# Sliding-window attention with global tokens, then a cosine MLP: the global score products of two pairs formed one slot earlier

## Chip, cores and metric

One of the cores of a Trainium2 chip runs the whole program. The metric is the device time of one execution in microseconds: 959.86 us, the median of three (959.55 to 961.06). The engines are named as the profile names them: PE (matmuls), PEld (PE's weight loads), DVE, ACT, POOL and SP, whose queue issues every DMA.

## What is computed

Eight batches, eight heads of 64, 512 local positions and 32 global ones. Global queries attend to everything; a local query sees the 32 global keys and the local keys within 32 positions. The attention output, 4352 rows of 512, goes through an MLP with the activation h·cos(h):

```python
s_g = scale * np.matmul(q_g, k_all.transpose(0, 1, 3, 2))
out_g = np.matmul(sm(s_g), v_all)
s_ll = np.where(np.abs(pos[:, None] - pos[None, :]) <= 32, s_ll, -1e9)
out_l = np.matmul(sm(np.concatenate([s_lg, s_ll], -1)), v_all)
h = x @ w_in
return (h * np.cos(h)) @ w_out
```

## The kernel before

Two heads make a *pair*, so a batch has four pairs. Two pairs, an even one and the odd one behind it, make a *group*, whose global queries are handled together.

The MLP is the backbone. Rows of x are taken in 17 chunks of 256; each chunk goes through eight *slots*, in each of which PE forms 256 columns of h (`m1_a`, L801, 24 matmuls into the PSUM tile `ph`) and multiplies the 256 columns of three slots earlier with w_out (`m2_a`, L860 to L862, 12 matmuls into `po`). Everything is held as the sum of two fp16 parts, hence three matmuls for each product. Between the two, ACT, DVE and POOL form the activation: `u` (L823 on ACT, L824 on DVE), its sine `w` (L425 on ACT), the square (L839 on POOL), `gf` (L841 on DVE), and its parts `gh` (L845 on ACT) and `gl` (L846 on POOL).

The attention of the batches is woven into these slots. A pair of batch 2 or later has a base slot t, 16 slots to a batch and four to a pair, and a table of offsets says what it does when:

- t-10: its queries and keys are loaded (`load_qk`, tile `qkr`, three buffers).
- t-7 and t-5: local scores (`sc_a`, L527). Each call makes two `ps` tiles, one for each head. DVE takes them out of PSUM, two instructions at L545 to a tile, with the row minimum `mn`.
- t-4: the exponentials on ACT (`sc_c`), and behind them those of the group's global scores `gt` if the pair is odd (`g_c`). Both go through L425, as the sine does, and each change between exponential and sine loads a table (ACT_TABLE_LOAD).
- t-3: the weights are scaled and split (L592 on ACT, L593 on DVE) into `planes`; of the global ones L709 to L721 make `planes_g`.
- t-1: SP transposes both by DMA (`pt` at L612, `ptg` at L725).
- t: the product with the values (`av_a`, 36 matmuls at L645 into `acc`), taken out by `xh` (L665, ACT) and `xl` (L666, DVE).
- t+2, odd pairs: the global product (`g_f`, L737, `gacc`), taken out at L750.
- The global scores of a group (`g_a`, L682, tile `gps`; taken out by DVE at L695) come in two calls, 288 and 256 keys wide, whose slots `s_gs0` and `s_gs1` set.

The tiles `ps`, `gps`, `acc`, `gacc` and a small one for the spread of a maximum (`pm`, L459) share one PSUM tag, `att`, with three buffers that are handed out in turn, in the order in which the program makes the tiles. So PE may write a tile only when the third tile before it has been taken out of PSUM.

The values of a whole batch come by one load (`load_v`, L446, tile `vr`, one buffer) at slot t-12 of its first pair, which is the slot in which L512 reads the last piece of the batch before. DVE then takes the maximum over them (`v_a`, L481, `vm`).

The calls of each slot are handed to a scheduler in the order of phases; it may move an instruction a little, so the order on each engine is read from the built program. Each engine executes its own list in that order.

Of the kernel before, what the change touches and what calls it, by code (L numbers as in the profile page):

```python
# [78 lines left out]
s_tr = -1  # L79
s_vd = -8  # L80
s_av = 0
s_gs0 = -6
s_gs1 = -4
s_gd = -3
s_ge = -1
s_gf = 2
# [998 lines left out]
```

## Time and profile before

| | before |
|---|---|
| median of 3 | 959.86 us |
| the profiled execution, and its span | 959.23 us, 957.5 us |
| PE busy | 909.4 us, 95% of the span |
| ACT busy | 668.4 us, 70% |
| DVE busy | 569.3 us, 59% |
| POOL busy | 399.7 us, 42% |
| DMA, the one queue of SP | 39.6% of 16 engines |

The profile is of one execution; its own time is 1.7 us over its span, and 0.6 us under the median. A page and several views of the trace are used: the timeline (start, duration, engine, line, operation, tiles, and in brackets idle time before it and what ended it), the waits (who waited for whom), the chain of work that ended last (start, duration, engine and line, with consecutive pieces merged), stretches of time with busy times by engine, and the DMAs. Busy times of PE are modelled ends of pipelined matmuls, so for PE the text uses the starts of matmuls.

### The profile page before, as it was taken

To read this page: it belongs to the slowest core of one execution; us is meant where nothing else is said; L and a number is where in the kernel's file an instruction comes from. 1 tells how busy PE (TensorE), PEld (TensorE's weight loads), DVE (VectorE), ACT (ScalarE), POOL (GpSimd) and SP (SyncE) were. 2 spreads that over 40 slices of the span, in tenths; PEclk is the share of its full clock that TensorE was granted. 3 is DMA by queue.
4 is the path that set the end of the run, shared out by engine and by line. 5 is a ranking of instruction groups with operands and counts; after the bars stand their busy time and mean duration, and the time that the engine had idled before them with its cause. 6 is when DMAs were issued, how large, how long until landed. Compare 5 with 4: busy or idle time off the path is not lost.

```text
span 957.5 us, 20487 instructions
## 1 busy us (share of the span) xinstructions
PE 909.4 (95%) x7963; PEld 604.0 (63%) x7963; DVE 569.3 (59%) x1544; ACT 668.4 (70%) x1435; POOL 399.7 (42%) x412
## 2 busy tenths in 40 slices
PE   6657989999999999999999999999999999999995
PEld 4446656656666666666666666666666666766663
DVE  5987978746565656566655656564746554423231
ACT  7886899957787677766777778777777775443341
POOL 5856654443334243434343333324343434444441
PEclk8667989999999999999999999999999999999998
DMA  9936167745232533545262725342443333000000
GB/s 371 386 121 198 34 163 162 152 111 125 49 108 43 157 63 71 108 122 111 56 122 50 183 46 129 46 146 46 119 61 71 81 68 58 23 1 23 1 24 22
DMA packets 155178, 96.44 MB, mean 101 GB/s; under 512 B 141000, under 2 KB 141128, under 8 KB 153288
## 3 DMA queue, kind: packets, MB, share of 16 engines
q1 hardware_dynamic: 155080, 95.13, 39.6%
q8 instruction: 62, 1.02, 0.4%
q14 instruction: 36, 0.29, 0.1%
HBM read 51.59 MB, written 8.91 MB: 63 GB/s over the span
## 4 chain that ended last, share of the span: by engine, by line
PE 51%; ACT 15%; DVE 11%; issue 9%; POOL 8%; DMA 5%; SPq 0%; ACTq 0%; POOLq 0%; DVEq 0%
PE ph L801 21%; PE po L861 8%; PE po L862 8%; PE po L860 8%; ACT t L425 4%; DMA vr<-v 3%; POOL w L839 3%; PE ps L527 3%; POOL gl L846 2%; ACT planes L592 2%; PE acc L645 2%; DVE gf L841 2%; ACT gh L845 2%; ACT L425 2%; POOL wi_l L213 2%
## 5 line engine op out<-in xcount | busy, mean ns | idle before, releaser
L801 PE MATMUL ph<-xh,wi_h 128*128 128x256 f16 x1024 | 280.7, 274 | 0.9 <-DVE gf L841 0.5
L801 PE MATMUL ph<-xl,wi_h 128*128 128x256 f16 x1024 | 279.8, 273 | 0.0
L801 PE MATMUL ph<-xh,wi_l 128*128 128x256 f16 x1024 | 279.8, 273 | 0.0
L846 POOL TENSOR_TENSOR gl<-gf,gh 128x512 f16<-128x512 f32 x136 | 163.4, 1202 | 237.1 <-ACT gh L845 237.0
L839 POOL TENSOR_TENSOR w<-w 128x512 f32<-128x512 f32 x136 | 143.6, 1056 | 259.1 <-ACT w L425 241.2
L801 PEld LDWEIGHTS <-wi_h 128*128 128x128 f16 x2176 | 205.9, 98 | 55.4 <-issue 18.8
L861 PE MATMUL po<-wo_hl,gh 128*128 128x512 f16 x544 | 206.7, 380 | 0.6 <-POOL wo_hl L213 0.6
L860 PE MATMUL po<-wo_hl,gh 128*128 128x512 f16 x544 | 204.7, 380 | 1.7 <-ACT wo_hl L239 1.7
L862 PE MATMUL po<-wo_hl,gl 128*128 128x512 f16 x544 | 206.3, 380 | 0.0
L845 ACT CAST gh<-gf 128x512 f16<-128x512 f32 x136 | 83.4, 615 | 112.8 <-DVE gf L841 112.7
L824 DVE SCALAR_TENSOR_TENSOR u<-u,cm,ph 128x512 f32<-128x512 f32 x136 | 101.1, 744 | 101.0 <-ACT u L823 101.0
L841 DVE SCALAR_TENSOR_TENSOR gf<-w,ph 128x512 f32<-128x512 f32 x136 | 93.1, 684 | 110.6 <-POOL w L839 110.1
L425 ACT ACTIVATE w<-u,ca 128x512 f32<-128x512 f32 x136 | 98.1, 722 | 84.4 <-DVE u L824 83.5
L425 ACT ACTIVATE t<-t,mn 128x192 f32<-128x192 f32 (+1 forms) x256 | 117.3, 463 | 18.5 <-DVE mn L545 18.1
L801 PEld LDWEIGHTS <-wi_l 128*128 128x128 f16 x1088 | 106.7, 98 | 13.4 <-issue 0.5
L823 ACT ACTIVATE u<-ph,cm 128x512 f32<-128x512 f32 x136 | 92.3, 679 | 25.2 <-PE ph L801 25.2
L593 DVE SCALAR_TENSOR_TENSOR planes<-t,sm,planes 128x192 f16<-128x192 f32 (+1 forms) x232 | 97.8, 481 | 12.0 <-ACT planes L592 11.2
L545 DVE CUSTOM_DVE_ANT_0 t<-ps,msk 128x192 f32<-128x192 f32 (+1 forms) x256 | 83.2, 367 | 18.0 <-PE ps L527 14.8
L862 PEld LDWEIGHTS <-gl 128*128 128x128 f16 x544 | 53.3, 98 | 63.1 <-issue 0.9
L592 ACT ACTIVATE planes<-t,sm 128x192 f16<-128x192 f32 (+1 forms) x232 | 86.3, 458 | 0.0
L861 PEld LDWEIGHTS <-gh 128*128 128x128 f16 x544 | 53.3, 98 | 51.5 <-issue 2.5
L860 PEld LDWEIGHTS <-gh 128*128 128x128 f16 x544 | 52.8, 98 | 51.4 <-issue 2.6
(149 smaller groups left out, 1098.5 us busy)
## 6 DMA issues: line engine op xcount, KB each, us to landing
qkr<-qf SPq DMA_DIRECT2D x31, 608.0 KB, 5.0
vr<-v SPq DMA_DIRECT2D x8, 1280.0 KB, 6.5
out<-o SPq DMA_DIRECT2D x34, 256.0 KB, 2.0
raw_wi<-wi SPq DMA_DIRECT2D x6, 1024.0 KB, 12.2
wo_hl<-wo SPq DMA_DIRECT2D x8, 512.0 KB, 12.7
raw_wm<-wo SPq DMA_DIRECT2D x8, 512.0 KB, 5.7
raw_wo<-wo SPq DMA_DIRECT2D x8, 512.0 KB, 4.4
raw_wi<-wi SPq DMA_DIRECT2D x4, 512.0 KB, 12.3
```

Source lines behind the costliest of these rows:

```text
L425: ins = nc.scalar.activation(*a, **k).ins
L592: a = nc.scalar.activation(hi, t[:, h], AF.Identity, scale=r)
L593: d = nc.vector.scalar_tensor_tensor(lo, t[:, h], r, hi, op0=ALU.mult, op1=ALU.subtract)
L801: nc.tensor.matmul(ph[:, a], w[:, kc, f], x[:, kc, q], start=first and ip == 0, stop=last and ip == 2, skip_group_check=True,)
L824: nc.vector.scalar_tensor_tensor(u, u, m, ph, op0=ALU.subtract, op1=ALU.subtract)
L839: nc.gpsimd.tensor_tensor(w, w, w, op=ALU.mult)
L841: nc.vector.scalar_tensor_tensor(gf, w, 0.5, st.pop(("ph", c, j)).rearrange("p a b -> p (a b)"), op0=ALU.subtract, op1=ALU.mult,)
L845: nc.scalar.copy(gh, gf)
L846: nc.gpsimd.tensor_tensor(gl, gf, gh, op=ALU.subtract)
L860: nc.tensor.matmul(po[k], gh[:, q], wo_h[:, f], start=(f == 0), stop=False)
L861: nc.tensor.matmul(po[k], gh[:, q], wo_l[:, f], start=False, stop=False)
L862: nc.tensor.matmul(po[k], gl[:, q], wo_h[:, f], start=False, stop=(f == NJ - 1))
```

## The change

```diff
 s_av = 0
-s_gs0 = -6
-s_gs1 = -4
+s_gs0 = -7
+s_gs1 = -5
 s_gd = -3
```

Both calls of `g_a` move one slot forward for batches 2 to 7, two groups each, twelve groups in all. At t-7 and t-5 they stand directly behind the odd pair's own local scores; until now the first stood alone in t-6, ahead of the global product of the group before, and the second stood in t-4 behind `av_a` of the even pair.

The tiles with the tag `att` are made in this order for an odd pair and the even one that follows (| between slots). Before: ps ps | gps0 gacc | ps ps | acc gps1, then ps ps | ps ps | acc. After: ps ps gps0 | gacc | ps ps gps1 | acc, then ps ps | ps ps | acc. Counted three back, the second global tile `gps1` took the buffer of the first `ps` of its t-5 pair before, and takes that of `gacc` now; `acc` took the buffer of `gacc` before, and takes that of that first `ps` now; `gps0` takes the buffer of the even pair's `acc` (slot t-8) in both.

On PE, in batch 3 at the first odd pair, this is the end of the t-4 slot before (`acc_3_0` is the even pair's product, `ps_3_1_2_0` in the next lists is the first of the two score tiles of t-5):

```order
L645 LDWEIGHTS vl_3_0_3757
L645 MATMUL acc_3_0_4412<-pt_3_0_4347,vl_3_0_3757 64x128
L682 MATMUL gps_3_0_1_4449<-qkr_3_0_3585 32x256 [waits DVE_49]
L682 MATMUL gps_3_0_1_4449<-qkr_3_0_3585 32x256
L682 MATMUL gps_3_0_1_4449<-qkr_3_1_3906 32x256 x2
L801 LDWEIGHTS wi_h_86
L801 MATMUL ph_4_4_4482<-xh_2_3046,wi_h_86 128x256
```

The product runs first, and the global scores behind it wait for DVE. After, in the t-5 slot of the same pair:

```order
L527 MATMUL ps_3_1_2_0_4341<-qkr_3_1_3906 128x224 [waits DVE_49]
L527 MATMUL ps_3_1_2_1_4342<-qkr_3_1_3906 128x224 [waits DVE_49]
L527 MATMUL ps_3_1_2_0_4341<-qkr_3_1_3906 128x192
L527 MATMUL ps_3_1_2_1_4342<-qkr_3_1_3906 128x192
L682 MATMUL gps_3_0_1_4347<-qkr_3_0_3585 32x256 [waits DVE_49]
L682 MATMUL gps_3_0_1_4347<-qkr_3_0_3585 32x256
L682 MATMUL gps_3_0_1_4347<-qkr_3_1_3906 32x256 x2
```

The same four matmuls now follow the local scores. One slot later PE begins the product after with this:

```order
L801 LDWEIGHTS wi_h_86
L801 MATMUL ph_4_4_4482<-xh_2_3046,wi_h_86 128x256
L645 LDWEIGHTS vh_3_0_3756 [waits DMAHW3_49]
L645 MATMUL acc_3_0_4418<-pt_3_0_4352,vh_3_0_3756 64x128 [waits DVE_49]
L645 LDWEIGHTS vh_3_0_3756
```

Its first matmul waits for DVE, where before it waited for an earlier matmul of PE.

On DVE, the list at that place before. `vm_4` is the maximum over the values of the next batch, and the two L545 instructions on `ps_3_1_2_0` are those that take the first score tile of t-5 out of PSUM:

```order
L786 TENSOR_SCALAR co_6_5489<-osc_96,pvs_98 128x1 [waits DVE_49,Activation_49]
L481 TENSOR_REDUCE vm_4_4864<-vr_4_4729 128x1 [waits DMAHW7_49]
L545 ISA t_3_1_2_4352,mn_3_1_2_4353<-ps_3_1_2_0_4341,msk_73 128x224 [waits PE_49]
L545 ISA mn_3_1_2_4353 128x1
L545 ISA t_3_1_2_4352,mn_3_1_3_4356<-ps_3_1_2_0_4341,msk_73 128x192
L545 ISA mn_3_1_3_4356 128x1
L841 SCALAR_TENSOR_TENSOR gf_4_2_4365<-w_4_2_4322,ph_4_2_4296 128x512 [waits Pool_49]
```

And after:

```order
L786 TENSOR_SCALAR co_6_5489<-osc_96,pvs_98 128x1 [waits DVE_49,Activation_49]
L481 TENSOR_REDUCE vm_4_4872<-vr_4_4729 128x1 [waits DMAHW7_49]
L545 ISA t_3_1_2_4357,mn_3_1_2_4358<-ps_3_1_2_0_4341,msk_73 128x224 [waits PE_49]
L545 ISA mn_3_1_2_4358 128x1
L545 ISA t_3_1_2_4357,mn_3_1_3_4361<-ps_3_1_2_0_4341,msk_73 128x192
L545 ISA mn_3_1_3_4361 128x1
L841 SCALAR_TENSOR_TENSOR gf_4_2_4371<-w_4_2_4322,ph_4_2_4296 128x512 [waits Pool_49]
```

These rows stand as they did: the maximum, which waits for a load, stays ahead of them. The instructions on `gps` (L695) move forward on DVE with their matmuls, each to a place behind the L545 instructions of its slot.

On ACT the exponential of the global scores moves ahead of the scaling. Before, in the same pair:

```order
L665 ACTIVATE xh_3_4455<-acc_3_0_4412,xs_90 128x512 [waits PE_49]
L592 ACTIVATE planes0_76<-t_3_1_0_4141,sm_3_1_4463 128x192 [waits DMAHW3_49,DVE_49,Activation_49]
...
L592 ACTIVATE planes3_82<-t_3_1_2_4352,sm_3_1_4463 128x192 [waits Activation_49]
L425 ACTIVATE gt_3_0_4221,gsm_3_0_4472<-gt_3_0_4221,gmn_3_0_4222 128x544 [waits DVE_49]
L425 ACT_TABLE_LOAD
L425 ACTIVATE w_4_3_4395<-u_4_3_4394,ca_4_4078 128x512 [waits Pool_49]
```

After:

```order
L425 ACTIVATE gt_3_0_4154,gsm_3_0_4472<-gt_3_0_4154,gmn_3_0_4155 128x544 [waits DVE_49]
L665 ACTIVATE xh_3_4455<-acc_3_0_4418,xs_90 128x512 [waits PE_49]
L425 ACT_TABLE_LOAD [waits DVE_49]
L425 ACTIVATE w_4_3_4401<-u_4_3_4400,ca_4_4078 128x512 [waits Pool_49]
L592 ACTIVATE planes0_76<-t_3_1_0_4146,sm_3_1_4463 128x192 [waits DMAHW3_49,DVE_49,Activation_49]
```

The exponential, the table load and the next sine now precede the eight scalings, so L593, L612 and the transposes of `planes` come later, and POOL's square of that sine earlier. On POOL the last step of `planes_g` (L721) moves ahead of that square, and on SP the transpose of `planes_g` moves ahead of the four of `planes`. The loads of queries and keys keep their place on SP; they wait for the last reader of their buffer, which is a call of `g_a`.

## The prediction

> **What bounds the kernel now.** The page comes first, for which engine has no idle time and where; then one stretch of time for the part that the change can reach.
>
> ```profile
> PE 909.4 (95%) x7963; PEld 604.0 (63%) x7963; DVE 569.3 (59%) x1544; ACT 668.4 (70%) x1435; POOL 399.7 (42%) x412
> PE   6657989999999999999999999999999999999995
> PEclk8667989999999999999999999999999999999998
> 205.00:815.00 610.00, 608.53 (x5587) 404.42 (x5585) 363.55 (x1011) 439.41 (x968) 225.85 (x202) 1.00 0.41 90
> ```
>
> From slice 7 on PE shows nine tenths or more in every slice, at a granted clock of nine tenths or more. The stretch from 205 to 815 us holds every moved instruction, from batch 2's first group to batch 7's last. In its 610 us PE is busy for 608.53 (the first pair of columns behind the stretch's length), ACT for 439.41, DVE for 363.55, at full clock. So whatever delays PE there delays the end, and a shorter wait of any other engine is worth nothing by itself.
>
> Next, the chain that ended last, for the prices of the pieces on PE (start, duration, engine and line; starts differ by up to 0.1 us from the timeline's):
>
> ```profile
> 226.51 1.29 PE acc L645 x36
> 227.80 0.57 PE gps L682 x8
> 228.37 2.73 PE ph L801 x24
> ...
> 251.34 1.29 PE acc L645 x36
> 252.63 2.73 PE ph L801 x24
> 257.95 0.90 PE ps L527 x8
> ...
> 264.23 0.62 PE gps L682 x8
> ```
>
> A product costs 1.29 us, whether `gps` or `ph` follows. `gps` costs 0.57 us behind the product, 0.62 where it stands alone ahead of the global product, and the local scores 0.90.
>
> Last, what PE waits for in the stretch, by the waits view, and the timeline of the four places (each even pair's `acc` at the first odd pair of batches 3 to 6; at the first place PE's bracket is missing because the wait is shorter than the modelled end):
>
> ```profile
> PE gps L682 <- DVE mn L545: 1.4, 3, 0.7
> ...
> 328.55 0.30 PE L645 MATMUL acc<-pt,vh 128*64 128x128 f16 x4
> 330.02 0.64 PE L682 MATMUL gps<-qkr 128*32 128x256 f32 x8
> 330.59 0.28 PE L801 MATMUL ph<-xh,wi_h 128*128 128x256 f16 x1
> ...
> 430.83 0.30 PE L645 MATMUL acc<-pt,vh 128*64 128x128 f16 x4
> 432.62 0.64 PE L682 MATMUL gps<-qkr 128*32 128x256 f32 x8 [0.43 <-DVE mn L545]
> ...
> 533.44 0.30 PE L645 MATMUL acc<-pt,vh 128*64 128x128 f16 x4
> 535.06 0.64 PE L682 MATMUL gps<-qkr 128*32 128x256 f32 x8 [0.26 <-DVE mn L545]
> ...
> 635.88 0.30 PE L645 MATMUL acc<-pt,vh 128*64 128x128 f16 x4
> 637.92 0.64 PE L682 MATMUL gps<-qkr 128*32 128x256 f32 x8 [0.68 <-DVE mn L545]
> 638.49 0.28 PE L801 MATMUL ph<-xh,wi_h 128*128 128x256 f16 x1
> ```
>
> That is PE's only wait in 610 us. From start to start the product takes 1.47, 1.79, 1.62 and 2.04 us at these places; less the clean 1.29, PE stands still for 0.18, 0.50, 0.33 and 0.75, together 1.76 us, with `gps1` at the head of its queue. The lost time is not made up: at the last place `ph` starts 0.57 us behind `gps`, as everywhere.
>
> DVE's timeline says why, and SP's and the DMAs' (KB, us to landing) say what is behind that:
>
> ```profile
> 326.56 2.82 DVE L481 TENSOR_REDUCE vm<-vr 128x1 f32<-128x2560 f32 x1 [3.05 <-DMA vr<-v]
> 329.30 0.38 DVE L545 CUSTOM_DVE_ANT_0 t<-ps,msk 128x224 f32<-128x224 f32 x1
> 329.60 0.35 DVE L545 CUSTOM_DVE_ANT_0 t<-ps,msk 128x192 f32<-128x192 f32 x1
> ...
> 320.42 0.33 SPq L446 DMA_DIRECT2D vr<-v  x1
> 321.86 1.70 SPq L877 DMA_DIRECT2D out<-o  x2
> 330.68 0.34 SPq L441 DMA_DIRECT2D qkr<-qf  x1
> ...
> vr<-v SPq DMA_DIRECT2D x1, 1280.0 KB, 6.1
> out<-o SPq DMA_DIRECT2D x2, 256.0 KB, 5.0
> ...
> out<-o SPq DMA_DIRECT2D x34, 256.0 KB, 2.0
> ```
>
> The load of the next batch's values lands at 326.5; DVE has stood in front of it for 3.05 us, reduces for 2.82, and only then empties the first score tile of t-5. Its second instruction ends at 329.95, and `gps1`, which has that tile's buffer, starts at 330.02.
>
> **The change part by part.**
>
> *The second call, t-4 to t-5.* By the turn of three buffers `gps1` no longer takes the late tile's buffer, and `acc` does; so the wait moves from behind the product to ahead of it. Behind `acc` stands all of PE. Nothing on the way to 329.95 is made earlier on DVE, ACT or SP, because the maximum, the load and what they wait for keep their places. So DVE frees the buffer when it did, and PE starts there a piece of 1.29 us instead of one of 0.57. Each place ends 1.29 - 0.57 = 0.72 us later, 4 x 0.72 = 2.9 us. Seen from the stop: `gps` is out of the way 0.57 us earlier in the queue, so `acc` would be ready at 328.55 + 0.57 - 0.05 = 329.07 and starts at 330.02: a stop of 0.95 for one of 0.18. At the four places 0.95, 1.27, 1.10 and 1.52. The other eight groups have that tile emptied long before, and their second call costs 0.57 on either side: nothing.
>
> *The first call, t-6 to t-7.* It leaves a group of its own (0.62) for one directly ahead of `ph`, which by the row at 227.80 takes 0.57: 0.05 less in twelve groups. In the four just counted the gain vanishes in the stop; in the other eight it is 0.4 us. The trace has no `gps` behind local scores at full clock. The change of operand shape there, 24 times, I bound by what the trace shows at such changes: the 0.05 between 0.62 and 0.57, taken off, and the same plus as much again, 0.10, on top: -1.2 to +2.4 us. I take 0, since a product costs 1.29 before `gps` and before `ph` alike.
>
> *New waits by the turn of buffers.* `gps0` comes a slot closer behind the product whose buffer it takes, and `gps1` takes that of `gacc`. Two of the tightest places:
>
> ```profile
> 357.22 0.75 DVE L666 SCALAR_TENSOR_TENSOR xl<-acc,xs,xh 128x512 f16<-128x512 f32 x1
> 361.07 0.23 PE L459 MATMUL pm_v<-d_v,ones 128*128 128x128 bf16 x1
> ...
> 680.30 0.28 DVE L750 TENSOR_SCALAR xg<-gacc,pvs 128x64 f32<-128x64 f32 x1
> 682.24 0.28 PE L801 MATMUL ph<-xh,wi_h 128*128 128x256 f16 x1
> ```
>
> `xl` is done at 357.97 and `gps0` would come at 361.07, behind the scores: 3.1 us spare. `xg` is done at 680.58 and `gps1` would come at 682.24: 1.7 spare. If that cover went, each group would pay what is missing. I take 0.
>
> *Order on ACT, DVE, POOL, SP.* For an odd pair the scaling now follows the global exponential, a table load and a sine:
>
> ```profile
> 335.98 0.74 ACT L425 ACTIVATE gt<-gt,gmn 128x544 f32<-128x544 f32 x1
> 336.83 1.28 ACT L425 ACT_TABLE_LOAD   x1
> 338.13 0.72 ACT L425 ACTIVATE w<-u,ca 128x512 f32<-128x512 f32 x1
> ...
> 384.53 5.35 SPq L612 DMA_TRANSPOSE pt<-planes  x4
> 404.49 0.30 PE L645 MATMUL acc<-pt,vh 128*64 128x128 f16 x4
> ```
>
> Together 2.7 us. The transposes of such a pair are issued by 389.9 and its product starts at 404.5, so 2.7 later still leaves them over 11 us to land. L841 now stands between two L593 and waits there for POOL; behind it hang the same transposes. The sine goes the other way, earlier by the length of the eight scalings, and its chain to `gl` with it: relief where PE does not wait. `planes_g` and its transpose are earlier too. All of it at nothing.
>
> *Loads of queries.* They wait for the last `g_a`, so they are issued nearer to 324 than to 330.7, while the values' load is still in flight. SP's order puts them behind it, and an `out` issued 1.4 us behind that load took 5.0 us where the median is 2.0: it queued behind, and took nothing from it. So 0.
>
> Sum: 2.9 - 0.4 = +2.5 us. The profiled execution would go from 959.23 to 961.7; the median stood 0.63 above it, which gives 962.4.
>
> **The rivals.**
>
> *The stop goes* (957.5). If the late tile were empty when `acc` comes, which needs DVE 0.95 to 1.52 us earlier at these places, the 1.76 us of waiting would vanish with nothing in its place, and 12 x 0.05 = 0.6 with it: 959.86 - 2.4. For it: DVE's list is lighter ahead of that point by one L695 of the slot before. Against: DVE idles there for 3.05 us until the load lands, so lighter work moves nothing. Chance 0.10.
>
> *The stop is made up* (959.3). If PE has room, a delay is recovered in the slots behind, and only 0.6 is left, as a gain. PEld's 404.42 of 610 us say that weights load in two thirds of the time. Against: `ph` follows `gps` by 0.57 whether or not PE has just stood still. Chance 0.20. The Trainium skill's page "Perfetto Trace Analysis", section "Identifying the Most-Contended Engine", holds that matmul busy time is no measure of how near TensorE is to its limit and that LDWEIGHTS busy share is; by that rule the 66% here leave room, and this rival would be the likeliest. The unchanged 0.57 behind a stop speaks against it here.
>
> *The loads share* (970). If the queries' loads took half the rate from 323.9 to 326.5, the values would land up to 2.6 us later at each place: 2.5 + 4 x 2.6 = 13, 973 at worst, 970 with a part of it. Against: the `out` that queued. Chance 0.05. The Trainium skill's page "DMA: Bandwidth & Descriptors", section "Issuing engines are not separate DMA queues", says that DMAs of different engines run on the same 16 engines and interleave; its section "Two DMAs through the same engine are not ordered" says that within one queue descriptors start in order. Every load here is SP's, and the late `out` sides with the second.
>
> **How the numbers follow.** The forecast has 0.65; its own range is 2.5 with -1.2 and +2.4: 961.2 to 964.8. A measurement of this kernel tells 0.2% (1.9 us, so 957.9 and 961.8) from no change. Of the 0.65 some 0.09 lie under 961.8: slower 0.56 + 0.05 = 0.61, the same 0.20 + 0.09 = 0.29, faster 0.10. The range takes in the second rival and the forecast, 959.2 to 964.8, and leaves out the first and third.
>
> **What would show it.** In the profile after, PE should wait at `acc` (L645) for `mn` of L545, at four places, near 1.0 to 1.5 us each, and no longer at `gps`; the product should follow DVE's second L545 by under 0.1 us. `gps` behind local scores should take 0.57. The values should still land some 6 us after issue. The prediction is wrong if PE does not stop at `acc`, if PE's other pieces are not where they were, or if the stop is followed by shorter pieces.

## The result, and the profile after

The changed kernel takes 965.36 us (median of 5, 963.92 to 965.65) against 959.55 (5 runs, 958.51 to 961.06) of the kernel before on the same chip: a ratio of 1.0057 [1.0042, 1.0071], slower by 5.8 us. Measured once more in a later group it took 963.88, a ratio of 1.0046 [1.0031, 1.0061], slower by 4.4. The forecast was +2.5, with 964.8 as the upper end of the range. The profiled execution took 965.36 us, its span 963.6.

First the page's totals, by engine (busy us, share of the span, instructions):

```profile
PE 912.8 (95%) x7963; PEld 606.5 (63%) x7963; DVE 580.9 (60%) x1544; ACT 667.3 (69%) x1435; POOL 403.1 (42%) x412
```

They tell little: PE's 95% are as before. The stretch of time that was read before tells more (columns as there):

```profile
205.00:815.00 610.00, 604.50 (x5532) 401.68 (x5531) 372.31 (x1006) 435.37 (x962) 228.06 (x202) 1.00 0.40 90
```

PE is busy for 604.50 of the 610 us where it was 608.53: it stands still four us more, at the same full clock. The waits view of the stretch says at what (waiter, who it waited for, us in total, times, longest):

```profile
PE pm_v L459 <- DVE mn L545: 5.2, 5, 1.2
PE acc L645 <- DMA qkr<-qf: 0.3, 1, 0.3
```

The wait at `gps` is gone, as forecast. The wait at `acc` is there, but small. The large one is at a tile that the prediction did not put into the turn of buffers: `pm`, the spread of the values' maximum, one matmul in each batch. This is PE's timeline at one of its five places, where in the kernel before the same matmul came directly behind the scores (the row at 361.07 in the prediction):

```profile
362.17 0.97 PE L527 MATMUL ps<-qkr 64*128 64x192 f32 x8
363.07 0.69 PE L682 MATMUL gps<-qkr 128*32 128x288 f32 x8
363.69 0.28 PE L801 MATMUL ph<-xh,wi_h 128*128 128x256 f16 x1
...
365.45 0.27 PE L801 MATMUL ph<-xl,wi_h 128*128 128x256 f16 x1
366.90 0.22 PE L459 MATMUL pm_v<-d_v,ones 128*128 128x128 bf16 x1 [1.17 <-DVE mn L545]
366.95 0.27 PE L801 MATMUL ph<-xh,wi_l 128*128 128x256 f16 x1
```

`ph`'s matmuls start 0.11 us apart, so PE stands for 366.90 - 365.45 - 0.11 = 1.34 us in the middle of `ph`. DVE at that time:

```profile
361.61 1.64 DVE L593 SCALAR_TENSOR_TENSOR planes<-t,sm,planes 128x192 f16<-128x192 f32 x3 [1.81 <-ACT planes L592]
...
363.77 1.83 DVE L593 SCALAR_TENSOR_TENSOR planes<-t,sm,planes 128x224 f16<-128x224 f32 x5
365.52 0.74 DVE L824 SCALAR_TENSOR_TENSOR u<-u,cm,ph 128x512 f32<-128x512 f32 x1
366.18 0.35 DVE L545 CUSTOM_DVE_ANT_0 t<-ps,msk 128x192 f32<-128x192 f32 x1
366.45 0.38 DVE L545 CUSTOM_DVE_ANT_0 t<-ps,msk 128x224 f32<-128x224 f32 x1
```

In this slot the tiles were made in the order ps ps pm before, and are made in the order ps ps gps0 pm now. Counted three back, `pm` took the buffer of the even pair's `acc`; now it takes that of the first `ps` formed just ahead of it, and starts 0.06 us after the end of DVE's second L545 on that tile (366.45 + 0.38 = 366.83). DVE comes late to it, since it waited for ACT's scalings of the pair before.

Next, DVE at the place that the prediction spoke of, ahead of `acc` at the first odd pair of batch 3:

```profile
328.58 2.82 DVE L481 TENSOR_REDUCE vm<-vr 128x1 f32<-128x2560 f32 x1 [2.89 <-DMA vr<-v]
331.31 0.38 DVE L545 CUSTOM_DVE_ANT_0 t<-ps,msk 128x224 f32<-128x224 f32 x1
...
331.62 0.35 DVE L545 CUSTOM_DVE_ANT_0 t<-ps,msk 128x192 f32<-128x192 f32 x1
...
331.90 0.68 DVE L841 SCALAR_TENSOR_TENSOR gf<-w,ph 128x512 f32<-128x512 f32 x1
...
333.49 1.22 DVE L453 TENSOR_SCALAR d_v<-ident,vm 128x128 bf16<-128x128 f32 x1
```

The maximum waits for the load and stands ahead of the late tile, as forecast; the tile is out at 331.97. (`d_v` at the end comes up again below.) The DMAs of that time (KB, us to landing):

```profile
vr<-v SPq DMA_DIRECT2D x1, 1280.0 KB, 6.1
qkr<-qf SPq DMA_DIRECT2D x2, 608.0 KB, 6.6
```

The values land 6.1 us after issue, as before; the queries' loads, issued now while they fly, do not slow them. PE at this place:

```profile
331.20 0.27 PE L801 MATMUL ph<-xh,wi_h 128*128 128x256 f16 x1
...
331.86 0.27 PE L801 MATMUL ph<-xh,wi_h 128*128 128x256 f16 x1
332.06 0.30 PE L645 MATMUL acc<-pt,vh 128*64 128x128 f16 x4
```

Seven matmuls of the next `ph` stand ahead of `acc`, and it starts 0.20 us behind the last of them. One of the runs below (after: gf, maximum, scores) has a product behind matmuls of `ph` too, in batch 2, where the tile had been out of PSUM for 2.6 us:

```profile
229.14 0.27 PE L801 MATMUL ph<-xh,wi_h 128*128 128x256 f16 x1
229.34 0.30 PE L645 MATMUL acc<-pt,vh 128*64 128x128 f16 x4
```

So 0.20 us is the plain step from `ph` to `acc`, and at this first place there is no stop that can be measured. At the second place of the changed kernel there is one:

```profile
435.30 0.27 PE L801 MATMUL ph<-xh,wi_h 128*128 128x256 f16 x1
435.82 0.30 PE L645 MATMUL acc<-pt,vh 128*64 128x128 f16 x4 [0.25 <-DMA qkr<-qf]
```

It is 435.82 - 435.30 - 0.20 = 0.32 us, and `acc` starts 0.06 us after DVE's second L545 there. (The bracket names what came last by the profile.)

The stops by places, start to start less the clean durations: `pm` 0.77, 1.34, 1.35, 1.22 and 1.36, together 6.04; `acc` 0, 0.32, 0 and 0.10, together 0.42; `gps` 0 for 1.76. That is +4.7. From the start of the 21st block of `ph` to the last product, which holds nearly all that moved, the trace of before has 812.42 - 228.31 = 584.11 us, that of after 818.53 - 229.72 = 588.81: +4.7 as well, so the stops account for this stretch in full. Ahead of it the two profiled executions differ by another 1.4 us, and behind it by nothing.

### The profile page after: what moved, and what is told of

It reads as the page before. It is cut to its first block, busy times and chain, and to the rows that moved or that the text cites. A ratio compares the mean times of both kernels' runs of the same rounds, so it can differ in the third digit from the quotient of the medians.

```text
span 963.6 us, 20510 instructions
## 1 busy us (share of the span) xinstructions
PE 912.8 (95%) x7963; PEld 606.5 (63%) x7963; DVE 580.9 (60%) x1544; ACT 667.3 (69%) x1435; POOL 403.1 (42%) x412
## 4 chain that ended last, share of the span: by engine, by line
PE 49%; ACT 16%; DVE 13%; issue 7%; POOL 7%; DMA 7%; SPq 0%; ACTq 0%; POOLq 0%; DVEq 0%
PE ph L801 20%; PE po L861 8%; PE po L862 8%; PE po L860 8%; ACT planes L592 5%; DMA vr<-v 5%; ACT t L425 3%; PE ps L527 2%; POOL w L839 2%; POOL gl L846 2%; PE acc L645 2%; DVE u L824 2%; DVE gf L841 2%; DVE vm L481 2%; ACT L425 2%
## 5 line engine op out<-in xcount | busy, mean ns | idle before, releaser
L846 POOL TENSOR_TENSOR gl<-gf,gh 128x512 f16<-128x512 f32 x136 | 165.4, 1217 | 285.6 <-ACT gh L845 285.5
L841 DVE SCALAR_TENSOR_TENSOR gf<-w,ph 128x512 f32<-128x512 f32 x136 | 93.0, 683 | 118.9 <-POOL w L839 118.8
L593 DVE SCALAR_TENSOR_TENSOR planes<-t,sm,planes 128x192 f16<-128x192 f32 (+1 forms) x232 | 105.3, 507 | 28.1 <-ACT planes L592 27.4
L545 DVE CUSTOM_DVE_ANT_0 t<-ps,msk 128x192 f32<-128x192 f32 (+1 forms) x256 | 83.2, 366 | 16.3 <-PE ps L527 12.6
```

Of the source, the lines that this page charges most:

```text
L593: d = nc.vector.scalar_tensor_tensor(lo, t[:, h], r, hi, op0=ALU.mult, op1=ALU.subtract)
L841: nc.vector.scalar_tensor_tensor(gf, w, 0.5, st.pop(("ph", c, j)).rearrange("p a b -> p (a b)"), op0=ALU.subtract, op1=ALU.mult,)
L846: nc.gpsimd.tensor_tensor(gl, gf, gh, op=ALU.subtract)
```

## The experiments

All kernels were timed beside the kernel before on the same chip. "Stops" are read from the profile as above, in us.

| kernel | median | ratio to before | pm | acc | gps |
|---|---|---|---|---|---|
| before | 959.4 to 960.4 | | 0 | 0 | 1.76 |
| after; again | 965.36; 963.88 | 1.0057 [1.0042, 1.0071]; 1.0046 [1.0031, 1.0061] | 6.04; 5.92 | 0.42; 0.89 | 0 |
| first call alone | 964.82 | 1.0055 [1.0042, 1.0067] | 5.90 | 0 | 0.99 |
| second call alone | 962.95 | 1.0035 [1.0022, 1.0047] | 0 | 5.27 | 0 |
| after, pm a slot later | 977.27 | 1.0182 [1.0164, 1.0200] | 0 | 14.35 | 0 |
| after, pm on ph's buffers | 971.59 | 1.0129 [1.0112, 1.0147] | 0 | 9.10 | 0 |
| before, pm a slot later | 965.93 | 1.0068 [1.0046, 1.0090] | 0 | 0 | 5.53 |
| before, maximum behind scores | 958.73 | 0.9983 [0.9974, 0.9992] | 0 | 0 | 0 |
| after, maximum behind scores | 958.77 | 0.9984 [0.9975, 0.9993] | 0.04 | 0 | 0 |
| second call, maximum behind scores | 958.32 | 0.9983 [0.9974, 0.9991] | 0 | 0 | 0 |
| pm on ph's buffers, maximum behind scores | 964.30 | 1.0045 [1.0030, 1.0059] | 0 | 0 | 0 |
| after: scores, maximum, gf | 959.92 | 1.0006 [0.9996, 1.0016] | 0.77 | 0 | 0 |
| after: gf, maximum, scores | 959.85 | 1.0001 [0.9993, 1.0010] | 1.71 | 0 | 0 |
| after, d_v one place forward | 965.09 | 1.0057 [1.0044, 1.0069] | 5.65 | 0.84 | 0 |
| first call: gf, maximum, scores | 960.75 | 1.0013 [1.0004, 1.0023] | 0.94 | 0 | 1.95 |
| first call: scores, maximum, gf | 958.80 | 0.9993 [0.9984, 1.0002] | 0.01 | 0 | 0 |

In all but three rows the stops are, within 0.1 us, what the stretch from the 21st block of `ph` to the last product takes over the 582.4 us that it has without stops (in the row "after: gf, maximum, scores" it holds one product more, 1.38 us). The two rows with the longest waits at `acc`, and the one with `pm` on `ph`'s buffers and the maximum behind the scores, have something beside; it is told where they come up.

**Each call alone, and pm out of the turn.** Theory A: the turn of buffers of `pm`. B: the prediction on record. C: the order on ACT, or something in the first 200 us.

The first call alone:

```diff
-s_gs0 = -6
+s_gs0 = -7
```

> Only the first global score call moves (t-6 to t-7); the second stays in t-4. Theory A (the small spread tile pm of L459, which shares the turn of three buffers, now takes the buffer of the scores formed just ahead of it and PE stops there): five stops at pm as in the changed kernel, 6.0 us, and 12 x 0.05 gained: +5.4 us against the kernel before, and gps keeps its four waits behind the product (1.8 us in all). Theory B (the recorded prediction: the cost is the product waiting at the second call's buffer): no second call moved, so -0.6 us and no stop at pm. Theory C (the cost comes from the exponential of the global scores standing earlier on ACT, or from the first 200 us): about 0.

Measured 964.82, +5.2, and the waits of the stretch, with `pm` again the tile that waits:

```profile
PE pm_v L459 <- DVE mn L545: 5.2, 4, 1.3
PE gps L682 <- DVE mn L545: 0.7, 3, 0.3
```

A was right: the call for which the prediction took -0.4 costs five us, all of it at `pm`. The second call alone:

```diff
-s_gs1 = -4
+s_gs1 = -5
```

> Only the second call moves (t-4 to t-5). Theory A: no stop at pm, since pm takes the even product's buffer as before; the product acc waits for the late score tile but stands behind seven matmuls of the next slot, so 0.8 us there in place of 1.8 at gps: -1.0 us. Theory B: +2.9 us, with PE stopped about 1 us at acc in four places. Theory C: the ACT order is that of the changed kernel here, so most of its extra time should show, +4 us.

Measured 962.95, +3.3:

```profile
PE acc L645 <- DVE mn L545: 3.3, 2, 1.7
PE acc L645 <- DMA qkr<-qf: 1.6, 1, 1.6
```

Here B had the place and the tile, and came near in size (2.9): `acc` waits for the late tile, 0.21, 1.66, 1.66 and 1.73 us behind seven matmuls of `ph`, 5.27 for the 1.76 at `gps`. By places B had 0.95, 1.27, 1.10 and 1.52, so part of the agreement is luck; the part on the prediction takes this up. (The second row is the same wait, put down to what ended last.) A had this too small. Alone the two cost 5.2 + 3.3 = 8.5, together 4.4 to 5.8: they do not add. The reason is in the times of L512, with which the last piece of the values is scaled and their buffer comes free for the next load: at the second of the places it ends 2.29 us ahead of the next block of `ph` with the second call alone, and 3.54 ahead in the changed kernel. While PE stands at `pm`, DVE and ACT go on, so load, maximum and late tile come earlier against PE, and the stop at `acc` shrinks by about as much.

Then the whole change, with `pm` kept from waiting in two ways:

```diff
-            at(t + s_v + 1, PG, v_b, b)
-            at(t + s_v + 1, PG2, v_c, b)
+            at(t + s_v + 2, PG, v_b, b)
+            at(t + s_v + 2, PG2, v_c, b)
```

> The changed kernel, with the matmul on the maximum of the values (v_b, L459) and what reads it (v_c) one slot later, so that pm is made behind gacc and takes the second score tile's buffer a slot after it was emptied. Theory A: the stops at pm go, 6.0 us; left are -1.8 at gps, +0.8 at acc and -0.6 of the first call: -1.6 us against the kernel before, 7 us under the changed kernel. Theory B: +2.5, since acc is untouched. Theory C: no change from the changed kernel, +4 to +6. Risk: gps1 of that pair now takes pm's buffer and may wait for L491.

```diff
-            early = name.startswith(("qk0", "v0"))
+            early = name[0] == "v" and name != "v1"
```

> The changed kernel with pm in the buffers of ph instead of those of the scores, for every batch from 2 on: both calls stay where the change put them and pm stays in its slot, only its buffer is another. Theory A: no stop at pm: -1.6 us against the kernel before, unless a ph tile now waits one slot sooner for gf (five places, under 1 us each). Theory B: +2.5. Theory C: +4 to +6.

Measured 977.27 and 971.59: every theory missed. The waits of the first:

```profile
PE acc L645 <- DVE mn L545: 14.1, 4, 5.0
```

`pm` no longer waits, and `acc` waits longer than ever. With `pm` at another place the scheduler also put the scalings of the values (L511 on ACT, L512 on DVE) at others. DVE with the second call alone:

```profile
319.49 0.69 DVE L841 SCALAR_TENSOR_TENSOR gf<-w,ph 128x512 f32<-128x512 f32 x1 [1.88 <-POOL w L839]
...
320.29 0.88 DVE L512 SCALAR_TENSOR_TENSOR vl<-vr,vs,vh 128x640 f16<-128x640 f32 x1
```

And with `pm` on `ph`'s buffers:

```profile
322.79 0.69 DVE L841 SCALAR_TENSOR_TENSOR gf<-w,ph 128x512 f32<-128x512 f32 x1 [2.26 <-POOL w L839]
...
323.59 0.87 DVE L512 SCALAR_TENSOR_TENSOR vl<-vr,vs,vh 128x640 f16<-128x640 f32 x1
```

The scores of t-5 start at 323.23 in the one and at 324.43 in the other, so L512 comes 2.94 us ahead of them in the one and 0.84 in the other, 2.1 later against PE. The two medians differ by 8.6, which is near to 4 x 2.1, but that is luck: at the four places L512 comes 2.10, -0.37, 1.04 and 1.05 us later, and the stops at `acc` grew by 2.24, -0.40, 1.04 and 0.95, together 3.8. For the kernel with `pm` a slot later (L512 at 325.23, the scores at 325.27) the shifts are 2.90, 2.10, 2.08 and 0.74, and the stops grew by 3.01, 1.93, 3.44 and 0.70, together 9.1; at the third place the values also came later, and the maximum started 7.92 us behind L512's end where it was 6.57 with the second call alone. Place by place, then, the stop moves with L512 and its load. The rest of what these two lie above the second call alone is not at `acc`. About 1.2 us (`pm` on `ph`'s buffers) and 2.0 us (`pm` a slot later) lie ahead of the 21st block of `ph`, and behind some of the long stops PE's granted clock was half, as here in the kernel with `pm` a slot later (columns as before, the clock third from the end):

```profile
549.58:553.00 3.42, 3.42 (x43) 2.88 (x40) 3.38 (x12) 3.42 (x13) 1.16 (x1) 0.50 0.00 0
```

At half the clock for 3.4 us PE loses 1.7 us; it happened twice in this trace and once in that of `pm` on `ph`'s buffers. The shifts suggested one chain for all variants, told in the next group. The same move of `pm` without the change was tried later:

> The kernel before with the spread of the values' maximum one slot later, as in the run of 977.3 that had this beside the change. Theory D (the chain from the last piece of the values to the late tile): if that move puts the last L512 later against PE here too, by x us, the four waits at gps grow by about x each, so for 2.9 us from 1.8 to some 12 us and the time to about 970, without anything of the change in it; if the last L512 stays where it was, 960, and the 977.3 came from the two edits together.

It took 965.93. L512 comes 1.4 us later against PE at the last three of the four places and not at the first; 3 x 1.4 = 4.2, and the waits at `gps` grew by 3.8, from 1.76 to 5.53; another 2.7 us lie ahead of the 21st block of `ph`. So a good part of what those edits cost is theirs and not the change's.

**The maximum behind the late score tiles.** Theory D: last piece of the values (L512), their load, the maximum (L481), the late tile: this chain sets PE's stops in every variant. E: the stop is only where a general lag shows, and comes back elsewhere. One order on DVE is added, from batch 3 on, and no wait is taken away:

```diff
+            b > 2 and tc.add_manual_dep(red.ins, st["late", b - 1, 1].name, order, reason="scores_first")
```

(`red` is the maximum, `late` the last L545 of the first odd pair of the batch before.) It goes into the kernel before, the changed kernel, the one with the second call alone, and the one with `pm` on `ph`'s buffers:

> The kernel before, with one order added: from batch 3 on the maximum over the values (L481) comes on DVE behind the last L545 of the first odd pair of the batch before, so it no longer stands ahead of the late score tile; PE's list is unchanged. Theory D (the chain last piece of the values, L512, then their load of 6.1 us, then the maximum of 2.8 us, then the late tile, sets PE's stops in every variant at these four places): gps no longer waits there, 1.76 us are gone, 959.7 - 1.8 = 957.9. Theory E (the stop is only where a general lag of DVE and ACT behind PE shows; taken from one tile it comes back at the next): 959.7, with a wait as long at another tile within a slot or two.

> The changed kernel with the same order added. Theory D: acc has no stop left at the four places (0.81 us less), the spread matmul pm keeps its five stops of 6.0 us, since nothing of its turn of buffers has changed: 965.4 - 0.8 = 964.6. Theory E: 965.4, the 0.81 us seen at another tile.

> The second call alone one slot sooner, with the same order added. Theory D: the four stops at acc (5.67 us in that kernel's profile) are gone, and nothing takes their place: 962.95 - 5.7 = 957.3, ahead of the kernel before. Theory E: 963, the stops at another tile. The prediction on record put the cost of the second call at these four places (2.9 us); if they go and the time falls under that of the kernel before by 1.8 to 2.4, it had the place and the cause right.

> The changed kernel with pm on the buffers of ph, and the same order added. That kernel without the order took 971.6, with four stops at acc of 9.5 us in its profile, which came in the place of pm's; ACT's scalings of the values (L511) stood there at another place, the last L512 ended 2.1 us later against PE than in the kernel with the second call alone, and its stops were 8.6 us longer, 4 x 2.1. Theory D: the stops at acc go, 971.6 - 9.5 = 962.1. Theory E: 971.6, and the lag of 2 us shows at another tile.

Measured 958.73, 958.77, 958.32 and 964.30, the first three under the kernel before by 1.6 to 2.1; there nothing comes back, and E falls. D is right for the first and the third. In the fourth, for which it gave 962.1, the stops at `acc` are gone too, but a part of them is seen elsewhere, as E had it:

```profile
PE ph L801 <- DVE gf L841: 2.8, 3, 1.1
```

That kernel's scalings of the values stand where the chain of `gf` runs late, and now PE waits for that. For the changed kernel D gave 964.6, since it took `pm`'s stops for a matter of their own; they went too. The same stretch of time in the changed kernel with this order:

```profile
205.00:815.00 610.00, 610.00 (x5602) 406.01 (x5601) 371.75 (x1012) 439.75 (x968) 230.28 (x204) 1.00 0.40 90
```

PE is busy for all of the 610 us. And DVE, ahead of `acc` in batch 3:

```profile
324.79 0.38 DVE L545 CUSTOM_DVE_ANT_0 t<-ps,msk 128x224 f32<-128x224 f32 x1
...
325.38 0.68 DVE L841 SCALAR_TENSOR_TENSOR gf<-w,ph 128x512 f32<-128x512 f32 x1
...
326.29 0.35 DVE L545 CUSTOM_DVE_ANT_0 t<-ps,msk 128x192 f32<-128x192 f32 x1
...
327.81 2.82 DVE L481 TENSOR_REDUCE vm<-vr 128x1 f32<-128x2560 f32 x1 [1.17 <-DMA vr<-v]
```

DVE does the four L545 and `gf` (L841) while the load flies; in the changed kernel the same five stood behind the maximum and its wait. At `pm`'s place, with an unchanged list on PE there, the second L545 now ends in time (PE):

```profile
364.64 0.27 PE L801 MATMUL ph<-xl,wi_h 128*128 128x256 f16 x1
364.75 0.22 PE L459 MATMUL pm_v<-d_v,ones 128*128 128x128 bf16 x1
```

One start follows the other by 0.11 us, without a stop. From the 21st block of `ph` to the last product it is 582.40 us here and 582.37 in the kernel before with the same order: with the stops gone the moved calls cost nothing and save nothing. These three, within 0.5 us of each other, and one of the kernels below (958.80) are the fastest of the study, ahead of both kernels.

**What makes DVE late to pm's tile.** In the changed kernel it is 38 us from the maximum to `pm`. Theory F: `gf` behind the maximum. G: `acc`'s stops, or its place behind seven matmuls. With the changed kernel repeated beside them, the two halves of the order (names shortened in both):

```diff
+            for x, y in ((red.ins, st["late", b - 1, 1]), (gf[2 * b - 4, 2], red.ins)):
+                tc.add_manual_dep(x, y.name, order, reason="scores_first")
```

and, in the other kernel,

```diff
+            for x, y in ((red.ins, gf[2 * b - 4, 2]), *((l545, red.ins) for l545 in late[b - 1, 1])):
+                tc.add_manual_dep(x, y.name, order, reason="scores_first")
```

The first puts scores, maximum and `gf` in this order on DVE, the second `gf`, maximum and scores.

> The changed kernel itself, unchanged, beside the others of this group. Its first median stood 5.8 us above the kernel before, of which the moved instructions account for 4.7 (from the 21st block of ph to the last product); the rest lies in the first 230 us, where the lists are the same. If that rest is the scatter of the first loads, the distance comes out nearer to 4.7 than to 5.8, 5.0 within 0.6; if something there belongs to the change, 5.8 again.

> The changed kernel with the maximum behind the late score tile as in the run that took 958.8, but with gf (L841) of that slot behind the maximum on DVE; PE's list is the same as in that run. Theory F (the five stops of 6 us at pm come 38 us earlier, from gf standing behind the maximum while that waits for the load: the activation chain then runs some 1.6 us late against PE for the next six slots, so DVE comes late to the score tile whose buffer pm takes): the lag comes back but for 0.6 us (two L545 that stood ahead of gf), pm stops again by 0.6 to 1.2 us at four or five places, acc does not stop: 958.8 + 3.5 = 962, between 960.5 and 964. Theory G (pm's stops come from acc's stops or from acc's place behind seven matmuls of ph): 958.8, no stop at pm.

> The other half: the changed kernel with gf ahead of the maximum on DVE, but the late score tiles still behind it (there the two first halves now come ahead of the two second, so the tile of acc's buffer is free 0.3 us later). Theory F: no stop at pm, stops at acc like those of the second call alone or 0.3 longer, 3.5 to 5 us in all against the run that took 958.8: 963. Theory G: stops at pm as well, since acc stops and stands behind matmuls of ph: 967 or more.

The repeated kernel stood 4.4 us above before, 5.0 within 0.6, so the first 5.8 held about one us of scatter: its 21st block of `ph` starts at 227.98, that of the first profile at 229.72, with the same lists up to there. The halves took 959.92 and 959.85, and both theories missed. Each half alone removes most of `pm`'s stops (0.77 and 1.71 are left of 6.04). In the second `acc` does not stop either; the scheduler put it behind 13 matmuls of `ph` there. But `d_v`, which took 1.22 us at four of five places in the changed kernel, took 0.28 in both halves, so two things had changed at once. Theory H: this `d_v`. I: the work queued behind the maximum. The first run moves `d_v` alone, the others move `gf` or the scores in the kernel with the first call alone, where `d_v` takes 0.28 anyway; PE's lists are unchanged in all three. The edit of the first (names shortened):

```diff
+            tc.add_manual_dep(l695[b - 1, 0, 1], d_v[b].name, order, reason="spread_first")
```

> The changed kernel with one order added on DVE: d_v (L453), which took 1.22 us at four of five places where it started just behind POOL's L846, goes one place forward, ahead of the L695 of the second call, as it stands before the change; PE's list is unchanged. Theory H (this stretch of 0.94 us is what makes DVE late to pm's tile): d_v takes 0.28 again, pm's stops fall from 6.0 to some 2.5 us, 964 to 965 becomes 961. Theory I (the work queued behind the maximum does it; the stretch lies beside other waiting): pm's stops stay between 5.5 and 6.0 us, 964.

> The first call alone one slot sooner (964.8, pm's stops 5.9 us, d_v 0.28 us), with gf ahead of the maximum on DVE and the score tiles behind it; PE's list is unchanged. Theory I: 0.68 us less behind the maximum at each place, pm's stops 4 x (1.47 - 0.68) = 3.2 us, 962. Theory H: nothing of d_v changes, pm's stops stay 5.9, 964.8.

> The same kernel with the score tiles ahead of the maximum and gf behind it. Theory I: four L545 of together 1.37 us less behind the maximum, pm's stops 4 x (1.47 - 1.37) = 0.4 us, the waits at gps (0.99) gone as well: 964.8 - 5.5 - 1.0 = 958.3. Theory H: only the waits at gps go, 963.8.

H falls: `d_v` took 0.28 again and the time stayed, 965.09. I has the cause: 960.75 and 958.80, for which it gave 962 and 958.3. It had the first too small, since `gf` ahead is worth more than its own 0.68 us (1.24 at each place). ACT shows why. With the first call alone:

```profile
326.50 0.69 ACT L823 ACTIVATE u<-ph,cm 128x512 f32<-128x512 f32 x1 [0.46 <-PE ph L801]
330.01 0.48 ACT L425 ACTIVATE t<-t,mn 128x224 f32<-128x224 f32 x1 [2.82 <-DVE mn L545]
...
330.89 0.62 ACT L845 CAST gh<-gf 128x512 f16<-128x512 f32 x1 [0.30 <-DVE gf L841]
331.42 0.48 ACT L425 ACTIVATE t<-t,mn 128x224 f32<-128x224 f32 x1
...
333.39 2.98 ACT L592 ACTIVATE planes<-t,sm 128x192 f16<-128x192 f32 x8
```

ACT stands in the middle of the exponentials for 2.82 us, waits once more for `gf`, and does the other three exponentials only then; the eight scalings start at 333.39. With the scores ahead of the maximum:

```profile
326.47 0.47 ACT L425 ACTIVATE t<-t,mn 128x224 f32<-128x224 f32 x1
...
328.27 0.67 ACT L823 ACTIVATE u<-ph,cm 128x512 f32<-128x512 f32 x1
330.87 0.62 ACT L845 CAST gh<-gf 128x512 f16<-128x512 f32 x1 [1.93 <-DVE gf L841]
...
331.98 2.97 ACT L592 ACTIVATE planes<-t,sm 128x192 f16<-128x192 f32 x8
```

The exponentials lie in that gap, and the scalings start at 331.98. What follows on ACT, DVE and POOL keeps this distance: in the 38th block of `ph` its `gf` starts 9.89 us behind its first matmul in the changed kernel and 8.29 with the maximum behind the scores, and so on, 1.5 to 1.6 apart, up to `pm`. The kernel before has this lag too (10.05 against 7.64): it did not pay at `pm`, because `pm` took another buffer.

## Why the prediction was wrong

- **What bounds the kernel** holds. PE has no room in this stretch: every stop lengthens the time, and none is made up (+4.7 by the stops, +4.7 by the trace). The last slice of PE's row, which the prediction counts among the full ones, shows five tenths and lies behind this stretch. The rival by which it would be made up did not happen. The Trainium skill, "Perfetto Trace Analysis", "Identifying the Most-Contended Engine", names MFU (the share of the peak matmul rate that the kernel reaches) and the LDWEIGHTS busy share as the measures of TensorE's headroom. PEld's 401.68 of 610 us are again 66% here, and the kernel still lost what PE waited, so in this case the share alone did not tell of room.
- **The step that failed is "New waits by the turn of buffers".** It went through `gps0` and `gps1` and took 0. `pm` has the same tag, was named in the description of the turn, and its row was quoted there as the clock for `gps0`'s slack; but the lists of tiles, written for a group in general, left it out, since only one slot in sixteen holds it. In that slot `gps0` comes between `ps ps` and `pm`, and `pm` gets a tile begun 3.4 us earlier. That is 6.0 us of stops which the sum lacks. With the second call's term 4.2 lower than forecast (0.42 - 1.76 = -1.3 for +2.9), and no gain of 0.4 from the first, this gives the 2.2 us by which the stretch was missed (4.7 for 2.5); the rest of the 3.0 us is not in the moved work, and lies within what the first part scatters. That the kernel came out slower, as forecast, is luck: in the whole change the call that was to cost the time saved 1.3.
- **The second call, +2.9**: right in place and cause where it stands alone (+3.3), and near in size by luck. `acc` stands behind seven matmuls of the next `ph` (the list of PE in the part on the change shows the last of them), which takes 4 x 0.76 = 3.0 us off the forecast stops; and at the last three places L512 ends only 0.82 us ahead of the scores of t-5, where it was 1.89 in the kernel before, which puts 3 x 1.07 = 3.2 on. Why it comes later there was not found out. In the whole change the stops at `acc` came to 0.42 and 0.89 instead of 4.84, less than the 1.76 that they replaced, since PE's stops at `pm` let the chain to the late tile catch up.
- **The first call, -0.4**: not there. The 0.62 and 0.57 are not a price of the place: after, the 288-key call takes 363.69 - 363.07 = 0.62 directly ahead of `ph` as well; it is the width. The change of operand shape behind the local scores, taken as 0, is 0.
- **"Nothing on the way is made earlier on DVE"** was right, and too narrow: the maximum in front of its load holds up not only the late tile but also `gf` and ACT's exponentials, and the lag of 1.6 us that follows reaches 38 us on. The prediction called ACT's and DVE's order "nothing" because PE did not wait for them there; it did not ask which tile would wait once the turn was changed.
- **Loads at 0**, and the rival in which they share: the values landed 6.1 us after issue in both; the rival did not happen. "The stop goes" did not either, until the maximum was moved by hand.

## What to carry to other kernels

When tiles share buffers in turn, write the whole turn before and after for every slot that differs, with the small tiles that come once in a while: a tile inserted into the turn gives each later one another predecessor. An instruction that waits for a load at the head of an in-order queue costs what is ready behind it, on that engine and on those that it feeds, even where the engine is half idle; here one order on DVE took 1.6 us off the kernel before and 6 to 7 off the changed one. And stops of one engine that hang on one late chain do not add: each gives the chain time, so undo them one by one and together.

## What the runs showed of the hardware

One DVE instruction took more than four times as long when it began just behind one of POOL's. The row of `d_v` in the changed kernel (durations in ns: least, median, most):

```profile
L453 DVE TENSOR_SCALAR d_v<-ident,vm x5: 279/1221/1227, 222.0 to 644.2; 128x128 bf16<-128x128 f32 x5
```

In the kernel before all five took 0.28. POOL beside the long one shown above, which runs from 333.49 to 334.71:

```profile
333.47 1.16 POOL L846 TENSOR_TENSOR gl<-gf,gh 128x512 f16<-128x512 f32 x1 [7.74 <-ACT gh L845]
```

It ends 0.08 us after POOL's. The Trainium skill, "SBUF — State Buffer", "Who interferes with whom", says that VectorE in a two-port mode, which `tensor_scalar` can enter, and GpSimd share a pair of SBUF ports as an exclusive lock, and that the one that comes later waits in full. This trace agrees with the wait; no run shows the mode. It cost little here, since moving `d_v` changed the time by nothing that can be measured.

The granted clock of PE was 1.00 from 205 to 815 us in both kernels, with stops of up to 1.4 us. In the kernel with `pm` a slot later it was 0.50 for 3.4 us from 549.58 and again from 655.40, at the ends of stops of 5.1 and 2.4 us, and in the one with `pm` on `ph`'s buffers from 334.41, at the end of one of 2.5 us. Behind stops of 3.2 and 3.6 us in the one and of 2.7 us in the other it stayed full, so the length of the stop alone does not decide it here.

Left open: what makes the first part scatter (the 21st block starts at 227.8 to 229.7 in kernels with nearly the same lists up to there, and at 230.4 to 231.5 in the four in which `pm` was moved).
